# Grouped-query attention on a cached K and V: units of two kv heads made units of four, with 2 MiB loads and VectorE transposes

## Chip, cores and metric

The kernel runs on one core of a Trainium2 chip. The metric is the device time of one execution in microseconds (us). Engines are named as in the profile: PE (TensorE, matmul), PEld (its weight loads), DVE (VectorE), ACT (ScalarE), POOL (GpSimd), SP (SyncE, which issues nearly all DMAs here).

## What is computed

```python
B, Sq, D = 8, 4, 512
Hq, Hkv, Sk, Dh = 32, 8, 2048, 128        # all bf16
q = (x @ wq).reshape(B, Sq, Hq, Dh).transpose(0, 2, 1, 3)
k = jnp.repeat(k_cache, 4, axis=1)        # k_cache, v_cache: (B, Hkv, Sk, Dh)
v = jnp.repeat(v_cache, 4, axis=1)
scores = jnp.einsum("bhqd,bhkd->bhqk", q, k) * (Dh ** -0.5)
p = softmax(scores, axis=-1)
o = jnp.einsum("bhqk,bhkd->bhqd", p, v)
out = o.transpose(0, 2, 1, 3).reshape(B, Sq, Hq * Dh) @ wo
```

Per kv head and batch there are only 16 queries (4 query heads of 4 tokens), so the 64 MiB of K and V cross from memory once and little is computed on each byte. wq and wo are 4 MiB each.

## The kernel before

**Units and loads.** A unit is one batch and a pair of kv heads, 32 units in all (L104). Its K tile and its V tile are 1 MiB each: 128 partitions, 64 for each of the two heads, and on each partition 32 consecutive keys of 128 elements, an 8 KiB run in memory (L108, L118). All loads are issued by SP in the order of the list `loads` (L148): K of unit u, then V of unit u-2, with small pieces of the first wo rows between them. Seven K buffers and six V buffers bound how far ahead `load_ready` (L160) may go. wo's first 1024 rows come in pieces of their own: `wo_e` (L128; eight pieces of five rows of 8 KiB), `wo_m` and `wo_n` (L135); the other 3 MiB come as `wo_sb` in eight loads after the last V (L141, called at w == NU-1-VB).

**K transposes.** `transpose_part` (L193) takes a quarter of a K tile. Two neighbouring bf16 values are seen as one fp32 word, so a 128x128 fp32 transpose on PE moves 128x256 values; four of them fill a PSUM tile, and DVE copies it to SBUF as `kt` (L200), 128x1024 bf16. Even and odd elements of a head's 128 dimensions then lie on 64 partitions each way, and the two kv heads of a unit lie on the two halves of the columns.

**q.** 128 matmuls of 32 columns (L220) make q for all heads, ACT scales it (L227), four matmuls with a selection matrix (L236) sort even and odd dimensions, and copies on DVE and ACT write the block-diagonal `q_bd` (L245).

**Scores and softmax.** `scores` (L254) runs 16 matmuls of 256 columns on four column groups of PE; ACT takes the exponential in two parts with a running sum each (L272). Nothing is subtracted first.

**Probabilities.** `probs_to_keys` (L277) transposes them back with four PE matmuls (L280), and two ACT copies out of PSUM (L286) place each head's 64 partitions into a zeroed `probs` tile, so that one value matmul serves both heads.

**Values.** `values` (L316) runs 32 matmuls of 32 columns with a 128x128 V block as weights (L321). `norms` (L293), every second unit, adds the sums over partitions with a matmul by ones (L303) and takes the reciprocal on DVE (L311); `finish` (L330) multiplies into `oT` (L332).

**Output.** `to_tokens` (L340) and `to_wo_rows` (L363) bring a group of heads into the order of wo's rows with PE transposes and copies (L345, L351, L367, L369), and `project` (L387) multiplies by wo (L397). Group 0 and group (1, 2) are done inside the loop; most of group 0's projection too. After the loop come the third group's transposes and 48 projection matmuls, then an ACT copy (L453) and two output DMAs.

**Order.** The order on every engine is the order of the program (`manual_schedule`, L71). The loop (after `project`) does, for step n: two K quarters of unit n, scores of n-1, the other two quarters, values, norms and finish of n-2, probs_to_keys of n-1.

Of the kernel before, what the change touches and what calls it, by code (L numbers as in the profile page):

```python
# [14 lines left out]
def kernel(  # L15
# [9 lines left out]
    nc = tc.nc  # L25
# [8 lines left out]
    G2 = Hkv // 2  # L34
    C = 2 * Sk // 128
    NQ = 2 * rep * Sq
    HQ = rep * Sq
    J = C // 2
    JT = J // 4
    HP = 2 * rep  # L40
    scale = float(Dh) ** -0.5
    NU = G2 * B
    KB = 7
    VB = 6
    A = 2
    KA = A + 1
    WR = HP
    DH = D // 2


    NE, WE, WM, WN = 40, 8, 5, 64
    assert NE * WE + 128 * WM + WN == HP * 128
    AX = mybir.AxisListType.X
    ADD = mybir.AluOpType.add
    assert Dh == 128 and C == 32 and NQ == 32 and G2 == 4

    const = ctx.enter_context(tc.tile_pool(name="const", bufs=1))
    wpool = ctx.enter_context(tc.tile_pool(name="wpool", bufs=1))
    kpool = ctx.enter_context(tc.tile_pool(name="kpool", bufs=KB))
    vpool = ctx.enter_context(tc.tile_pool(name="vpool", bufs=VB))  # L60
    ktpool = ctx.enter_context(tc.tile_pool(name="ktpool", bufs=6))
    small = ctx.enter_context(tc.tile_pool(name="small", bufs=2))
    psum_k = ctx.enter_context(tc.tile_pool(name="psum_k", bufs=3, space=bass.MemoryType.PSUM))
    psum_s = ctx.enter_context(tc.tile_pool(name="psum_s", bufs=1, space=bass.MemoryType.PSUM))
    psum_t = ctx.enter_context(tc.tile_pool(name="psum_t", bufs=1, space=bass.MemoryType.PSUM))
# [4 lines left out]

    order = ctx.enter_context(tc.manual_schedule())  # L71


    pad0 = const.tile([128, 192], BF16, name="pad0")
    wo_e = const.tile([64, WE, D], BF16, name="wo_e")
    wo_n = const.tile([WN, D], BF16, name="wo_n")
    wo_m = const.tile([128, WM, D], BF16, name="wo_m")
    x_sb = const.tile([T, D], BF16, name="x_sb")
    wq_sb = wpool.tile([128, R, HqDh], BF16, tag="w", name="wq_sb")
    xT_sb = const.tile([128, R, T], BF16, name="xT_sb")  # L80
    qT_all = const.tile([128, G2, B, HP, Sq], BF16, name="qT_all")


    q_bd = const.tile([128, G2, 2, B, 2, 2, HQ], BF16, name="q_bd")
    pick = const.tile([128, 2, 2, Dh // 2], BF16, name="pick")
    ident4 = const.tile([128, 128], FP32, name="ident4")

    groups = [(0,), (1, 2), (3,)]
    oT = [const.tile([128, HP, len(ps), B, Sq], BF16, name=f"oT{ps[0]}") for ps in groups]
    out_sb = const.tile([2 * T, DH], BF16, name="out_sb")  # L90
    oP12 = const.tile([128, WR, 2, T], BF16, name="oP12")
    nat_sb = const.tile([2 * T, HP * 128 + 24 * WE], BF16, name="nat_sb")
    oP3 = const.tile([128, WR, T], BF16, name="oP3")
    oP = [None, oP12[:, :, 0, :], oP12[:, :, 1, :], oP3[:, :, :]]
    oE = const.tile([64, WE, T], BF16, name="oE")
    oM = const.tile([128, WM, T], BF16, name="oM")
    oN = const.tile([WN, T], BF16, name="oN")
    ident = const.tile([128, 128], BF16, name="ident")
    by_q = const.tile([128, HQ], FP32, name="by_q")
    ones = const.tile([128, 128], FP32, name="ones")  # L100
    pad = const.tile([128, 96], BF16, name="pad")
    probs = [const.tile([128, C, 2, HQ], BF16, name=f"probs{i}") for i in range(3)]

    units = [(p, b) for p in range(G2) for b in range(B)]  # L104
    ks = [None] * NU
    vs = [None] * NU

    def load_k(u):  # L108
        if u >= NU:
            return  # L110
        p, b = units[u]
        ks[u] = kpool.tile([128, C, Dh], BF16, tag="k_sb", name="k_sb")
        nc.sync.dma_start(  # L113
            ks[u][:, :, :],
            k_cache[b, 2 * p : 2 * p + 2].rearrange("g (s c) d -> (g s) c d", c=C),
        )

    def load_v(u):  # L118
        if u >= NU:
            return  # L120
        p, b = units[u]
        vs[u] = vpool.tile([128, C, Dh], BF16, tag="v_sb", name="v_sb")
        nc.sync.dma_start(
            vs[u][:, :, :],
            v_cache[b, 2 * p : 2 * p + 2].rearrange("g (s c) d -> (g s) c d", c=C),
        )

    def load_wo_e(i):  # L128

        hi, m = divmod(i, 4)  # L130
        rows = wo[: NE * WE, :].rearrange("(q r) j -> q r j", r=WE)
        a, b = hi * 32 + m, hi * NE // 2 + m
        nc.sync.dma_start(wo_e[a : a + 17 : 4, :, :], rows[b : b + 17 : 4, :, :])

    def load_wo_m():  # L135
        nc.sync.dma_start(wo_n[:, :], wo[HP * 128 - WN : HP * 128, :])
        nc.sync.dma_start(
            wo_m[:, :, :], wo[NE * WE : HP * 128 - WN, :].rearrange("(q r) j -> q r j", r=WM)
        )

    def load_wo(p, r0, n):  # L141
        rows = wo[p * HP * 128 : (p + 1) * HP * 128, :].rearrange("(q r) j -> q r j", r=WR)
        nc.sync.dma_start(wo_sb[:, p - 1, r0 : r0 + n, :], rows[:, r0 : r0 + n, :])

    load_k(0)
    nc.sync.dma_start(wq_sb[:, :, :], wq.rearrange("(p r) n -> p r n", r=R))
    nc.sync.dma_start(x_sb[:, :], x.flatten_outer_dims())
    loads = []  # L148
    for u in range(NU + KA):
        if 1 <= u <= 8:  # L150
            loads.append(("e", u - 1))
        if 0 < u < NU:
            loads.append(("k", u))
        if u == NU + 2:
            loads.append(("m", 0))
        if u >= KA - 1 and u - KA + 1 < NU:
            loads.append(("v", u - KA + 1))
    loads.reverse()

    def load_ready(nk, nv):  # L160

        while loads:
            kind, u = loads[-1]
            if kind in "em":
                loads.pop()
                load_wo_e(u) if kind == "e" else load_wo_m()
                continue
            if u >= (nk + KB if kind == "k" else nv + VB):
                return
            loads.pop()  # L170
            (load_k if kind == "k" else load_v)(u)

    nc.gpsimd.memset(wo_e[:, :, :], 0.0)
    load_ready(0, 0)

    make_identity(nc, ident[:])
    make_identity(nc, ident4[:])
    for e in range(2):
        for g in range(2):
            nc.vector.tensor_copy(  # L180
                out=pick[:, e, g, :], in_=ident[:, :].rearrange("d (k e) -> d e k", e=2)[:, e, :]
            )
    nc.vector.memset(q_bd[:, :, :, :, :, :, :], 0.0)
    for t in probs:
        nc.vector.memset(t[:, :, :, :], 0.0)
    nc.vector.memset(ones[:, :], 1.0)
    nc.vector.tensor_reduce(
        out=by_q[:, :], in_=ident4[:, :].rearrange("p (c q) -> p q c", q=HQ), axis=AX, op=ADD
    )

    kt = {}

    def transpose_part(u, t):  # L193
        kp = psum_k.tile([128, JT, 128], FP32, tag="k", name="kp")
        k4 = ks[u][:, :, :].rearrange("s c d -> s (c d)").bitcast(FP32)
        for j in range(JT):
            w = (t * JT + j) * 128
            nc.tensor.transpose(kp[:, j, :], k4[:, w : w + 128], ident4[:, :])  # L198
        k_t = ktpool.tile([128, JT, 128, 2], BF16, tag="kt", name="kt")
        nc.vector.tensor_copy(  # L200
            out=k_t[:, :, :, :].rearrange("k j s e -> k (j s e)"),
            in_=kp[:, :, :].rearrange("k j s -> k (j s)").bitcast(BF16),
        )
        kt[(u, t)] = k_t
# [281 lines left out]
```

## Time and profile before

| what | us |
|---|---|
| time, median of 3 runs | 190.58 |
| lowest and highest run | 188.97, 190.89 |
| span of the profiled execution | 187.5 |
| PE, PEld, DVE, ACT busy in it | 143.8, 119.1, 108.6, 69.5 |
| bytes moved by DMA | 75.92 MB, mean 405 GB/s |

The span runs from the first to the last instruction of one profiled execution; the run's own time contains that and what lies around it, and is not listed for the profiled execution itself. Busy times overlap between engines. The chain that ended last is followed back from the last instruction: each step names what released it. The slices cut the span in 40 equal parts, each digit being tenths of busy time.

### The profile page before, as it was taken

To read this page: it belongs to the slowest core of one execution; us is meant where nothing else is said; L and a number is where in the kernel's file an instruction comes from. 1 tells how busy PE (TensorE), PEld (TensorE's weight loads), DVE (VectorE), ACT (ScalarE), POOL (GpSimd) and SP (SyncE) were. 2 spreads that over 40 slices of the span, in tenths; PEclk is the share of its full clock that TensorE was granted. 3 is DMA by queue.
4 is the path that set the end of the run, shared out by engine and by line. 5 is a ranking of instruction groups with operands and counts; after the bars stand their busy time and mean duration, and the time that the engine had idled before them with its cause. 6 is when DMAs were issued, how large, how long until landed. Compare 5 with 4: busy or idle time off the path is not lost.

```text
span 187.5 us, 5636 instructions
## 1 busy us (share of the span) xinstructions
PE 143.8 (77%) x2474; PEld 119.1 (63%) x2474; DVE 108.6 (58%) x217; ACT 69.5 (37%) x202; POOL 4.6 (2%) x9
## 2 busy tenths in 40 slices
PE   0516799977879988898788888787787888878493
PEld 0506488866658867786676766566676677667272
DVE  0850698757527766577565657575565666663120
ACT  2001664553324444153344444433344443425200
POOL 8100000000000000000000000000000000000000
PEclk9975999999969999999999999999999999999759
DMA  5999999999999999999999999999999999999970
GB/s 204 467 447 379 421 435 416 425 426 425 425 425 428 421 423 423 430 421 428 425 428 421 428 425 418 428 428 418 430 426 419 425 426 428 419 426 408 409 277 12
DMA packets 10984, 75.92 MB, mean 405 GB/s; under 512 B 1288, under 2 KB 1448, under 8 KB 2600
## 3 DMA queue, kind: packets, MB, share of 16 engines
q1 hardware_dynamic: 10912, 75.55, 96.2%
q8 instruction: 19, 0.31, 0.6%
q14 instruction: 5, 0.04, 0.1%
q10 hardware_dynamic: 48, 0.02, 0.0%
HBM read 75.53 MB, written 0.03 MB: 403 GB/s over the span
## 4 chain that ended last, share of the span: by engine, by line
DMA 92%; PE 6%; SPq 0%; issue 0%; ACT 0%; DVE 0%
DMA k_sb<-in_k_cache_dram 58%; DMA v_sb<-in_v_cache_dram 18%; DMA wo_m<-in_wo_dram 9%; DMA wq_sb<-in_wq_dram 8%; PE out_ps L397 3%; PE kp L198 1%; PE o_ps L321 1%; PE nat L345 0%; SPq L113 0%; PE perm L367 0%; PE s_ps L261 0%; ACT out_sb L453 0%; DVE oT L332 0%
## 5 line engine op out<-in xcount | busy, mean ns | idle before, releaser
L200 DVE COPY kt<-kp 128x1024 bf16<-128x1024 bf16 x128 | 82.3, 685 | 38.6 <-PE kp L198 38.4
L198 PE MATMUL kp<-ident,k_sb 128*128 128x128 f32 x512 | 71.3, 284 | 24.3 <-DMA k_sb<-in_k_cache_dram 22.7
L198 PEld LDWEIGHTS kp<-ident,k_sb 128*128 128x128 f32 x512 | 57.0, 144 | 36.0 <-issue 18.5
L286 ACT COPY probs<-pt 64x512 bf16<-64x512 bf16 x64 | 37.1, 580 | 53.1 <-PE pt L280 52.7
L272 ACT ACTIVATE s_sb<-s_ps 128x256 bf16<-128x256 f32 x64 | 24.0, 380 | 34.1 <-PE s_ps L261 21.7
L321 PE MATMUL o_ps<-probs,v_sb 128*128 128x32 bf16 x1024 | 30.7, 177 | 2.0 <-DMA v_sb<-in_v_cache_dram 1.2
L321 PEld LDWEIGHTS <-v_sb 128*128 128x128 bf16 x1024 | 29.8, 96 | 3.7 <-DMA v_sb<-in_v_cache_dram 2.8
L261 PE MATMUL s_ps<-kt,q_bd 128*32 128x256 bf16 x512 | 20.9, 282 | 0.0
L261 PEld LDWEIGHTS <-q_bd 128*32 128x32 bf16 x512 | 10.6, 95 | 6.2 <-issue 5.4
L311 DVE RECIPROCAL r_sb<-l_ps 128x64 f32<-128x64 f32 x16 | 8.9, 557 | 8.6 <-PE l_ps L303 8.6
L272 ACT ACTIVATION_READ_ACCUMULATOR s_sb<-s_ps 128x1 f32 x64 | 12.7, 198 | 0.0
L280 PE MATMUL pt<-ident,s_sb 128*128 128x128 bf16 x128 | 12.3, 218 | 0.0
L303 PE MATMUL l_ps<-by_gq,ones 128*128 128x64 f32 x32 | 6.9, 297 | 5.2 <-DVE by_gq L296 5.2
L332 DVE TENSOR_TENSOR oT<-o_ps,r_sb 128x32 bf16<-128x32 f32 x32 | 6.1, 191 | 6.5 <-PE o_ps L321 5.9
L303 PEld LDWEIGHTS l_ps<-by_gq,ones 128*128 128x128 f32 x32 | 4.8, 188 | 6.7 <-DVE by_gq L296 4.9
L280 PEld LDWEIGHTS <-s_sb 128*128 128x128 bf16 x128 | 8.8, 104 | 0.2 <-ACT s_sb L272 0.2
L227 ACT ACTIVATE qT_all<-psq 128x256 bf16<-128x256 f32 x4 | 1.5, 385 | 16.6 <-PE psq L220 16.6
L245 DVE CAST q_bd<-pse 64x512 bf16<-64x512 f32 x4 | 2.6, 682 | 4.3 <-PE pse L236 4.3
L296 DVE TENSOR_TENSOR by_gq<-l_sb,by_q 128x64 f32<-128x64 f32 x16 | 3.5, 216 | 2.1 <-ACT s_sb L272 2.1
L397 PE MATMUL out_ps<-wo_sb,oP 128*32 128x256 bf16 x48 | 4.4, 336 | 0.0
L210 PE MATMUL xtp<-ident,x_sb 32*128 32x32 bf16 x4 | 0.3, 192 | 4.8 <-DMA x_sb<-in_x_dram 4.8
L453 ACT CAST out_sb<-out_ps 64x256 bf16<-64x256 f32 x1 | 0.4, 366 | 9.6 <-PE out_ps L397 9.6
(45 smaller groups left out, 43.0 us busy)
## 6 DMA issues: line engine op xcount, KB each, us to landing
k_sb<-in_k_cache_dram SPq DMA_DIRECT2D x32, 1024.0 KB, 19.6
v_sb<-in_v_cache_dram SPq DMA_DIRECT2D x32, 1024.0 KB, 13.3
wq_sb<-in_wq_dram SPq DMA_DIRECT2D x1, 4096.0 KB
wo_sb<-in_wo_dram SPq DMA_DIRECT2D x4, 512.0 KB
wo_sb<-in_wo_dram SPq DMA_DIRECT2D x4, 256.0 KB, 8.1
wo_m<-in_wo_dram SPq DMA_DIRECT2D x1, 640.0 KB
wo_e<-in_wo_dram SPq DMA_DIRECT2D x8, 40.0 KB
wo_n<-in_wo_dram SPq DMA_DIRECT2D x1, 64.0 KB, 18.2
```

The source lines that it names most:

```text
L198: nc.tensor.transpose(kp[:, j, :], k4[:, w : w + 128], ident4[:, :])
L200: nc.vector.tensor_copy(out=k_t[:, :, :, :].rearrange("k j s e -> k (j s e)"), in_=kp[:, :, :].rearrange("k j s -> k (j s)").bitcast(BF16),)
L261: nc.tensor.matmul(s_ps[t * 32 : (t + 1) * 32, :, g, :], lhsT=q_bd[:, p, e, b, g, :, :], rhs=kt[(u, t)][:, :, g * 64 : (g + 1) * 64, e], s ...
L272: nc.scalar.activation(out=s_sb[:, :, g, :], in_=s_ps[:, :, g, :], func=EXP, accum_out=l_sbs[u][:, u % 2, g : g + 1])
L280: nc.tensor.transpose(pt[:, j, :], s_sbs[u][:, j, :, :].rearrange("q g s -> q (g s)"), ident[:, :])
L286: nc.scalar.copy(out=pr[rows, :, g, :], in_=pt[rows, :, :].rearrange("s j (c q) -> s (j c) q", q=HQ),)
L296: nc.vector.tensor_tensor(out=by_gq[:, :, :, :], in0=l_sbs[u][:, :, :].unsqueeze(3).to_broadcast([128, 2, 2, HQ]), in1=by_q[:, :].unsqueez ...
L303: nc.tensor.matmul(l_ps[:, :, :].rearrange("d u q -> d (u q)"), lhsT=ones[:, :], rhs=by_gq[:, :, :, :].rearrange("k u g q -> k (u g q)"), ...
L311: nc.vector.reciprocal(r_sb[:, :, :], l_ps[:, :, :])
L321: nc.tensor.matmul(o_ps[:, :], lhsT=vs[u][:, 2 * (t * JT + j) + c, :], rhs=pr[:, i, :, :].rearrange("s g q -> s (g q)"), start=(i == 0), s ...
L332: nc.vector.tensor_tensor(out=oT[(p + 1) // 2][:, :, (p == 2) * 1, b, :], in0=o_pss[u][:, :].rearrange("d (h s) -> d h s", h=HP), in1=r_sb ...
L397: nc.tensor.matmul(out_ps[half * T : (half + 1) * T, :], lhsT=o, rhs=w[:, half * DH : (half + 1) * DH], start=(p == 0 and r == 0), stop=(p ...
```

## The change

A unit becomes one batch and four kv heads, 16 units (two groups of heads p, eight batches). A head has 32 partitions instead of 64, and 64 consecutive keys on each: runs of 16 KiB, and K and V loads of 2 MiB. All large tiles (K, V, two halves of wq, two halves of wo) share one pool of nine slots of 2 MiB; a load may be issued when a slot has been counted free. The separate first pieces of wo go; wo is loaded after the last V, in two and four loads. The last V comes in two loads.

The work goes by half units h (32 of them; 32 keys of each partition): 16 K transposes in four groups, 8 score matmuls of 512 columns, one exponential of 512 columns. The probabilities are turned by one DVE transpose of 32x32 blocks from SBUF to SBUF, and four ACT copies from SBUF, one per head, place them in `probs`. Value matmuls have 64 columns, 32 per half unit, and both halves add into one PSUM tile. `norms` runs once per unit with two matmuls. q is made by 32 matmuls with 512 columns, scaled by ACT and DVE, and sorted by 16 PE transposes. `to_tokens` and `to_wo_rows` run once per group of 16 heads: for the first after unit 7, for the second after the loop. The whole projection, 64 matmuls in two PSUM tiles on four column groups, comes after that; the last copy becomes a DVE addition of the two.

The core of the diff:

```diff
-    G2 = Hkv // 2
-    C = 2 * Sk // 128
+    G = 4
+    GP = Hkv // G
+    S = 128 // G
+    C = Sk // S
+    J = C // 2
+    JH = J // 2
+    CH = C // 2
+    NU = GP * B
+    NH = 2 * NU
+    SLOTS = 9
...
-    kpool = ctx.enter_context(tc.tile_pool(name="kpool", bufs=KB))
-    vpool = ctx.enter_context(tc.tile_pool(name="vpool", bufs=VB))
-    ktpool = ctx.enter_context(tc.tile_pool(name="ktpool", bufs=6))
+    kv = ctx.enter_context(tc.tile_pool(name="kv", bufs=SLOTS))
+    ktpool = ctx.enter_context(tc.tile_pool(name="ktpool", bufs=2))
...
+    def load_kv(to, of, u, parts, name):
         p, b = units[u]
+        to[u] = slot([128, C, Dh], name)
+        rows = of[b, G * p : G * (p + 1)].rearrange("g (s c) d -> (g s) c d", c=C)
+        n = C // parts
+        for i in range(parts):
+            cs = slice(i * n, (i + 1) * n)
+            nc.sync.dma_start(to[u][:, cs, :], rows[:, cs, :])
...
+    def load_wo(p):
+        wos[p] = slot([128, WR, D], "wo_sb")
+        rows = wo[p * HP * Dh : (p + 1) * HP * Dh, :].rearrange("(q r) j -> q r j", r=WR)
+        cuts = [0, 8, 16] if p < GP - 1 else [0, 8, 12, 14, 16]
+        for a, z in zip(cuts, cuts[1:]):
+            nc.sync.dma_start(wos[p][:, a:z, :], rows[:, a:z, :])
+
+    loads = []
+    for u in range(1, NU):
+        loads.append(lambda u=u: load_kv(ks, k_cache, u, 1, "k_sb"))
+        loads.append(lambda u=u: load_kv(vs, v_cache, u - 1, 1, "v_sb"))
+    loads.append(lambda: load_kv(vs, v_cache, NU - 1, 2, "v_sb"))
+    for p in range(GP):
+        loads.append(lambda p=p: load_wo(p))
...
+    def scores(h):
+        u, hh = divmod(h, 2)
         p, b = units[u]
+        s_ps = psum_s.tile([128, JH, S], FP32, tag="s", name="s_ps")
+        for e in range(2):
+            for g in range(G):
+                nc.tensor.matmul(
+                    s_ps[g * 32 : (g + 1) * 32, :, :],
+                    lhsT=q_bd[:, p, e, g, b, :, :],
+                    rhs=kts[h][:, :, g * S : (g + 1) * S, e],
...
+        nc.scalar.activation(
+            out=s_sbs[h][:, :, :], in_=s_ps[:, :, :], func=EXP, accum_out=l_sbs[u][:, hh : hh + 1]
+        )
...
+    def to_keys(h):
+        pTs[h] = small.tile([128, JH, 2, HQ], BF16, tag="pT", name="pT")
+        nc.vector.transpose(
+            out=pTs[h][:, :, :, :].rearrange("s j c q -> s (j c q)"),
+            in_=s_sbs[h][:, :, :].rearrange("q j s -> q (j s)"),
+        )
+
+    def by_head(h):
+        pr = probs[h % len(probs)]
+        for g in range(G):
+            rows = slice(g * 32, (g + 1) * 32)
             nc.scalar.copy(
                 out=pr[rows, :, g, :],
+                in_=pTs[h][rows, :, :, :].rearrange("s j c q -> s (j c) q"),
             )
...
+    def to_tokens(p, half):
+        n = HP // 2
+        nat = psum_l.tile([T, n, Dh], BF16, tag="l", name="nat")
+        for i in range(n):
             nc.tensor.transpose(
...
+        (nc.scalar.copy if half else nc.vector.tensor_copy)(
+            out=nat_sb[:, half * n * Dh : (half + 1) * n * Dh],
+            in_=nat[:, :, :].rearrange("t h d -> t (h d)"),
+        )
+
+    def to_wo_rows(p):
+        perm = psum_l.tile([128, WR, T], BF16, tag="l", name="perm")
...
+    def odd(p, r):
+        return r % 2 == 1 and (p < GP - 1 or r < WR - 4)
...
+            o, at = (out_odd, 2 * T) if odd(p, r) else (out_ps, 0)
...
+    for h in range(1, NH + 2):
+        fresh = 2 <= h < NH
+        if fresh:
+            transposes(h, 0)
+            transposes(h, 1)
+        if h - 1 < NH:
+            scores(h - 1)
+        if fresh:
+            transposes(h, 2)
+        if h == 1:
+            load_ready(2)
+        if h >= 2:
+            if h % 2 == 1:
+                norms((h - 2) // 2)
+            values(h - 2, 0)
+        if h - 1 < NH:
+            to_keys(h - 1)
+        if fresh:
+            transposes(h, 3)
+        if h >= 2:
+            values(h - 2, 1)
+        if h - 1 < NH:
+            by_head(h - 1)
+        if h >= 2 and h % 2 == 1:
+            u = (h - 2) // 2
+            finish(u)
+            if units[u] == (0, B - 1):
+                for half in range(2):
+                    to_tokens(0, half)
+                to_wo_rows(0)
+
+        load_ready((h < NH and h % 2 == 1) + (h >= 2 and h % 2 == 1))
...
+    to_tokens(1, 0)
+    to_tokens(1, 1)
+    to_wo_rows(1)
+    out_ps = psum_e.tile([2 * T, DH], FP32, tag="e", name="out_ps")
+    out_odd = psum_o.tile([128, DH], FP32, tag="o", name="out_odd")
+    project(0, 0, WR)
+    project(1, 0, WR - 4)
+    nc.scalar.copy(out=odd_sb[:, :], in_=out_odd[2 * T :, :])
+    project(1, WR - 4, 4)
...
+    nc.vector.tensor_tensor(out=out_sb[:, :], in0=out_ps[:, :], in1=odd_sb[:, :], op=ADD)
```

## The prediction, as it was put on record

> **What bounds the kernel now.** I read the busy table and the slices first, then the chain that ended last, then the groups of instructions, and last the end of the run in short windows. Busy table, slices and chain shares of the page:
>
> ```profile
> PE 143.8 (77%) x2474; PEld 119.1 (63%) x2474; DVE 108.6 (58%) x217; ACT 69.5 (37%) x202; POOL 4.6 (2%) x9
> ...
> DMA  5999999999999999999999999999999999999970
> GB/s 204 467 447 379 421 435 416 425 426 425 425 425 428 421 423 423 430 421 428 425 428 421 428 425 418 428 428 418 430 426 419 425 426 428 419 426 408 409 277 12
> ...
> DMA 92%; PE 6%; SPq 0%; issue 0%; ACT 0%; DVE 0%
> ```
>
> The DMA engines are full from the second slice to the last but one, at about 425 GB/s, and no compute engine is over 77%: the loads set the pace. The chain in order of time shows how the run ends:
>
> ```profile
> 159.04 17.10 DMA wo_m<-in_wo_dram
> 176.14 0.04 issue
> 176.18 1.58 PE out_ps L397 x12
> 177.76 0.98 PE o_ps L321 x32
> ...
> 178.77 0.20 DVE oT L332
> ...
> 181.50 2.98 PE out_ps L397 x40
> ...
> 184.51 0.37 ACT out_sb L453
> ```
>
> The last bytes of wo land at 183.3 (the trace's packet records), the last matmul ends at 184.5: compute runs out just behind the loads. What counts is therefore when the last loads land, and how long the work behind the last V tile is. The groups that price it (columns: line, engine, operation, tiles, shapes, count | busy us, mean ns | idle before, releaser):
>
> ```profile
> L200 DVE COPY kt<-kp 128x1024 bf16<-128x1024 bf16 x128 | 82.3, 685 | 38.6 <-PE kp L198 38.4
> ...
> L286 ACT COPY probs<-pt 64x512 bf16<-64x512 bf16 x64 | 37.1, 580 | 53.1 <-PE pt L280 52.7
> L272 ACT ACTIVATE s_sb<-s_ps 128x256 bf16<-128x256 f32 x64 | 24.0, 380 | 34.1 <-PE s_ps L261 21.7
> L321 PE MATMUL o_ps<-probs,v_sb 128*128 128x32 bf16 x1024 | 30.7, 177 | 2.0 <-DMA v_sb<-in_v_cache_dram 1.2
> ...
> L311 DVE RECIPROCAL r_sb<-l_ps 128x64 f32<-128x64 f32 x16 | 8.9, 557 | 8.6 <-PE l_ps L303 8.6
> ```
>
> ACT's probs copies have long idle time in front (52.7 us on PE's transposes), so today they are cheap. And the end in windows (span, then busy time and count by engine, granted clock, DMA share, GB/s):
>
> ```profile
> 181.50:183.00 1.50, 1.50 (x18) 1.11 (x20) 0.29 (x1) 0.00 (x0) 0.00 (x0) 0.55 0.35 132
> 183.00:184.60 1.60, 1.46 (x28) 1.07 (x22) 0.00 (x0) 0.09 (x1) 0.00 (x0) 1.00 0.02 8
> ```
>
> 18 projection matmuls took 1.5 us at a granted clock of 0.55, 28 took 1.6 us at 1.00: 83 against 57 ns each.
>
> **Loads: what the change gains.** In the trace's packet records an 8 KiB packet takes 309 ns, a 32 KiB one (wq) 1213 ns, 4 KiB 159, 2 KiB 84, and the 4-byte completion of each load 9 ns. No 16 KiB load is shown; between the 8 and 32 KiB rows it is 309 + 904/3 = 610 ns (bounds 606, half of 1213, and 618, twice 309). A 2 MiB load puts 8 such packets on each of 16 engines: 8 x 610 + 9 = 4.89 us, against 2 x (8 x 309 + 9) = 4.96 now. Over 32 of them that is 2.3 us. wo loses its pieces on five engines (wo_e) and its 5 and 1 KiB rows: per engine 24 x 309 + 8 x 159 + 16 x 84 + 54 = 10.1 us against 10.3 now. Per engine after: 32 x 4.89 + 9.78 (wq) + 10.1 = 176.4, plus 1.3 for the 19 instruction and 11 table fetches, from 2.15 (first packets) gives 179.9, and the slowest engine 0.9 later: 180.8. The same sum for the kernel before gives 182.5 where the records show 181.4 to 183.3. So the last byte lands some 2.5 us earlier.
>
> SP's queue: landing takes 19.6 us now because eight 1 MiB loads stand in line. After, SP waits in order for a slot (K of unit u+5 stands behind V of u+3), nine slots hold up to 40 us of loads; unless compute falls some 25 us behind, no load starts late, and this costs nothing.
>
> **Steady work.** A half unit (one pass h) has 4.89 us of load. PE: 16 transposes 1.7 us (8 in 0.85), 0.17 gap, scores 0.57 (the same columns on four column groups), values 32 x 28 ns = 0.9 us by the L321 row with 32 columns. With 64 columns a value matmul can cost no less than 28 ns and no more than the 55 ns of L280's 128 columns; I take 29, near the lower row, since the same 128x128 weights are loaded and 128 columns hide that load entirely. The 128 L280 transposes go. Odd passes add two norm matmuls (0.32) and PE's wait for by_gq, which now sits behind three kt copies on DVE; values and the next transposes are queued behind it: some 0.8 to 1.0 us. A pair: 4.0 + 4.85 = 8.8 us of the loads' 9.8. DVE: 8 x 0.645 + two 32x32 transposes + 0.28 + 0.56 + 0.23. No DVE transpose is in the trace; for 512 columns the bounds are 0.49 (the 512-word memset, L185) and 1.33 (two of L245's casts of 512 columns, 0.68); I take 0.66, one pass, near that cast: 7.6 us per pair. ACT: one exp of 512 columns, 0.58 like L286's 512 columns and 0.11 of the 0.20 us sum read that follows and is not overlapped, 0.69; and four copies of 32x512. Bounds for a copy: 0.29 (half the area of L286) and 0.65; time goes by columns (128x256 takes 0.38, 64x512 takes 0.58), so 0.60 each, 2.4 per pass, where two copies of 0.585 do it now: 6.2 us per pair. Beside the loads that is hidden; behind the last loads it is not.
>
> [...]
>
> to_tokens(0) and to_wo_rows(0) come inside pass 17 with PE waiting for each copy: 5.8 us, regained at 1.0 per pair by unit 13 or 14: free, but all spare is used. q: wq's second half lands at 17.5 (15.3 now), q ends near 25 (22.5 now); the same slack hides it. POOL's memsets end before 8 us, under the first loads.
>
> **The end.** V14 lands at 2.15 + 33 x 4.93 + 0.7 = 165.5 (4.93 with fetches). PE takes it in pass 30 and ends that at 166.9. Pass 31: two groups of transposes 0.9 and scores(30) 0.6 to 168.4, a third group 0.45 and 0.25 until it is in PSUM, its copy 0.65 to 169.75, by_gq 0.28 to 170.05, the norm matmuls 0.62 to 170.7, reciprocal 0.56 to 171.25, to_keys(30) 0.66 to 172.0 (exp(30) was done at 169.3). From there ACT carries it in order: by_head(30) 2.4 to 174.4, exp(31) to 175.1, to_keys(31) to 175.8, by_head(31) to 178.2, then values(31) 1.1 and finish 0.25: 179.6. V15 (170.5) and wo wait long in SBUF. Then, one after another, as psum_l has one buffer: eight transposes 0.9, DVE copy 0.68 (L351), eight more 0.9, ACT copy of 1024 columns 1.0 (0.58 + 512 columns at 0.20 per 256), 16 transposes 1.2, copy 0.43 (L369), hops: 5.3. Then all 64 projection matmuls, none issued earlier: 36 ns each on four groups at full clock (L261's pace) to 83 ns; PE idled before it, so the clock is low first: 57 ns, 3.6 us (2.3 to 5.3). Latency 0.3, add 0.4, output 2.7 (184.9 to 187.55 now). 179.6 + 12.3 = 191.9. The wo_m wait (2.5 us) and the probs transposes are gone, but lie inside what this replaces.
>
> The profiled span is 187.55, so +4.4. Its own time is not listed; the median of the runs, 190.58, stands 3.0 over the span (1.4 to 3.3 by run), so 195.0.
>
> **Rivals.** (a) Values do not hide their 64 columns: at 55 ns PE needs 10.5 us per pair against 9.8, the lag of pass 17 is never regained, the end is at 201.4, time 204.4; at 42 ns 194, time 197. For: PE then leads; against: L280's four matmuls of 128 columns follow each other at 55 ns with a new 128x128 load each, so the load (28 ns) lies beside the matmul, not behind it. Chance 0.13. (b) DVE's transposes take two passes, 1.33: DVE has 8.9 us of work per pair, and since the fourth kt copy stands behind the transpose and the next scores behind that copy, the pair takes over 10; end 203, time 206. Against: one pass is the plain case. Chance 0.06.
>
> [...]
>
> (c) ACT's copies go by area, 0.29: finish at 177.4, span 189.7, time 192.7, and with the projection at 36 ns 191.4: within 1%. Against: the two ACT rows. Chance 0.12. (d) The loads set the end, faster: the last bytes at 180.8 plus the last matmuls 0.3, latency, add and output give 184.3, time 187.3. It decides if the work from V14 to the last matmul takes under 15.6 us; the rows give 23. For it: before, compute ended 1.2 us behind the loads. Chance 0.07. My case keeps 0.62.
>
> **Numbers.** About 1% (1.9 us) is what a measurement of this kernel can tell from no change. Faster holds (d), 0.07; same holds (c), whose two times lie on both sides of that bound, 0.12; slower holds my case, (a) and (b), 0.81. The range runs from (c) with the fast projection, 191.4, to four fifths of the way into (a), 50 ns a matmul, span 197 and time 200; it leaves out (d), the upper part of (a) and (b), some 0.2. My own case alone runs from 193 (load packets at 606 ns, projection at full clock) to 199 (copies at 0.65, values at 38 ns, projection at 83 ns).
>
> **What would show it.** Right: 16 KiB packets near 610 ns and the last wo byte near 181; by_head near 0.6 each and PE idle on ACT in passes 32 and 33; finish near 179.6; 64 projections after it. Wrong: PE with no idle time from pass 18 on (a), a transpose over 0.9 (b), ACT copies near 0.3 (c), or the last matmul within 2 us of the last landing (d).

## The result, and the profile after

The changed kernel takes 198.62 us (median of 4 runs, 197.85 to 201.96) against 190.63 us (188.97 to 190.89) for the kernel before in the same comparison: a ratio of 1.042, 95% interval 1.036 to 1.049. It is slower, and 3.6 us over the forecast of 195.0, inside the range. The profile shown here is that of a second set of runs of the same kernel, whose execution took 198.25 us with a span of 196.5: in the first profile (span 200.1) the 16 KiB packets took about 680 instead of 611 ns between 20 and 66 us, a slow stretch that some of the traces below have too. The ratios, and the times of the experiments, leave out executions that are longer by some per cent, as some of either kernel are.

Busy table, granted clock, DMA share, rate and chain shares of the page of the changed kernel:

```profile
PE 146.2 (74%) x2036; PEld 113.1 (58%) x2036; DVE 124.0 (63%) x223; ACT 111.4 (57%) x202; POOL 3.8 (2%) x11
...
PEclk9999757699999999999999789999999999997558
DMA  6999999999999999999999999999999999995000
GB/s 200 434 437 427 434 430 427 427 427 430 437 424 429 425 427 430 434 420 430 430 434 427 434 430 427 430 424 434 427 425 430 432 427 415 422 424 233 0 3 8
...
PE 48%; ACT 19%; DVE 18%; DMA 8%; issue 4%; SPq 1%; ACTq 0%; DVEq 0%
```

Before, the DMA engines were full to the end and 92% of the chain was DMA. Now they run dry in the 37th of 40 slices, the last three hold no load at all, and DMA is 8% of the chain. The last byte of wo lands at 181.4, against 183.3 before, and the run goes on for 15 us after it. The granted clock of the last four slices is 0.5 to 0.8; before, it also fell near the end (0.7 and 0.5 in two slices), but was back at 1.00 for the last 28 matmuls.

The same middle stretch of both, span of the window, then busy time of PE, PEld, DVE, ACT and POOL, granted clock, DMA share and GB/s; first the changed kernel, then the kernel before:

```profile
60.00:160.00 100.00, 84.73 (x1258) 66.85 (x1255) 77.22 (x139) 69.32 (x126) 0.00 (x0) 0.98 1.01 429
```

```profile
60.00:160.00 100.00, 83.95 (x1472) 70.05 (x1465) 65.32 (x132) 40.96 (x125) 0.00 (x0) 1.00 1.01 425
```

The loads run 1% faster. PE has 214 matmuls fewer and is as busy as it was; DVE has 12 us more in these 100, ACT 28 more. What the change took from PE (the 128 probs transposes) went to DVE and ACT.

The groups that the prediction had to price without a row (busy us, mean ns, idle before):

```profile
L245 ACT COPY probs<-pT 32x512 bf16<-32x512 bf16 x128 | 78.8, 616 | 39.2 <-DVE pT L236 38.1
...
L280 PE MATMUL o_ps<-probs,v_sb 128*128 128x64 bf16 x1024 | 41.1, 195 | 8.5 <-ACT probs L245 6.3
...
L236 DVE STREAM_TRANSPOSE pT<-s_sb 128x512 bf16<-128x512 bf16 x32 | 21.9, 685 | 11.6 <-ACT s_sb L228 11.6
```

A copy of 32 partitions by 512 columns takes ACT 0.62 us, the transpose takes DVE 0.68; the value matmul's 195 ns overlap, as 16 of them follow each other in 0.47 (29 ns each).

PE's waits from 60 to 168 us, engine and line, then what it waited for, in total, times, longest:

```profile
PE l_ps L262 <- DVE by_gq L254: 10.8, 11, 1.0
PE o_ps L280 <- ACT probs L245: 3.1, 10, 0.3
...
```

No V tile and no K tile is in that list: in this stretch every load is there before PE asks for it. The values of the even passes start at 63.54, 72.54, 81.53, 90.52 and 99.52, that is 8.99 us a pair, PE's own pace, while the loads take 9.95 (V8 to V14). And the pass in which the first 16 heads are turned (PE's timeline: start, us, what, idle before):

```profile
99.52 0.63 PE L280 MATMUL o_ps<-probs,v_sb 128*128 128x64 bf16 x16 [0.31 <-ACT probs L245]
...
106.68 0.62 PE L301 MATMUL nat<-ident,oT 128*32 128x128 bf16 x8 [0.52 <-DVE oT L290]
108.07 0.61 PE L301 MATMUL nat<-ident,oT 128*32 128x128 bf16 x8 [0.77 <-DVE nat_sb L306]
109.77 1.17 PE L315 MATMUL perm<-ident,nat_sb 32*128 32x32 bf16 x16 [1.09 <-ACT nat_sb L306]
...
114.47 0.63 PE L280 MATMUL o_ps<-probs,v_sb 128*128 128x64 bf16 x16
```

From 99.52 to 114.47 are 14.95 us, 5.96 more than a pair. Last, the end of the chain in order of time (start, us, what):

```profile
174.27 0.58 DVE pT L236
...
174.87 0.62 ACT probs L245
...
176.76 0.62 ACT probs L245
...
177.39 0.60 ACT s_sb L228
...
178.24 0.72 DVE pT L236
...
180.87 0.62 ACT probs L245
...
181.53 1.88 PE o_ps L280 x32
...
183.71 1.05 PE nat L301 x8
...
186.57 1.01 ACT nat_sb L306
...
188.80 0.33 PE out_ps L326 x2
...
191.91 0.86 PE out_ps L326 x8
```

The kernel before started its last values at 177.7 and had only the last projections behind the last byte (183.3); now there is one long series of pieces on ACT, DVE and PE in turn. V14 lands at about 167.0 (166.9 in this trace's landing records; in two kernels below PE waits for it until 167.0), so this series is 29.5 us long, and the last wo byte (181.4) falls into the middle of it.

### The profile page after: what moved, and what is told of

It reads as the page before. It is cut to its first block, busy times and chain, and to the rows that moved or that the text cites. A ratio compares the mean times of both kernels' runs of the same rounds, so it can differ in the third digit from the quotient of the medians.

```text
span 200.1 us, 4726 instructions
## 1 busy us (share of the span) xinstructions
PE 146.9 (73%) x2036; PEld 113.7 (57%) x2036; DVE 124.9 (62%) x223; ACT 111.4 (56%) x202; POOL 3.8 (2%) x11
## 4 chain that ended last, share of the span: by engine, by line
DMA 45%; PE 29%; ACT 11%; DVE 10%; issue 2%; SPq 1%; DVEq 0%
DMA v_sb<-in_v_cache_dram 37%; PE kp L159 11%; ACT probs L245 9%; DMA x_sb<-in_x_dram 8%; PE o_ps L280 6%; DVE kt L160 3%; PE l_ps L262 3%; PE s_ps L218 3%; DVE pT L236 3%; DVE r_sb L270 2%; PE out_ps L326 2%; PE nat L301 2%; PE perm L315 1%; ACT nat_sb L306 1%; PE psq L180 1%
## 5 line engine op out<-in xcount | busy, mean ns | idle before, releaser
L245 ACT COPY probs<-pT 32x512 bf16<-32x512 bf16 x128 | 78.8, 616 | 42.9 <-DVE pT L236 41.8
L159 PE MATMUL kp<-ident,k_sb 128*128 128x128 f32 x512 | 79.9, 294 | 8.6 <-DMA k_sb<-in_k_cache_dram 8.6
L280 PE MATMUL o_ps<-probs,v_sb 128*128 128x64 bf16 x1024 | 41.3, 195 | 12.0 <-ACT probs L245 5.2
L280 PEld LDWEIGHTS <-v_sb 128*128 128x128 bf16 x1024 | 39.4, 101 | 15.9 <-issue 9.2
L236 DVE STREAM_TRANSPOSE pT<-s_sb 128x512 bf16<-128x512 bf16 x32 | 21.9, 684 | 11.3 <-ACT s_sb L228 11.3
L228 ACT ACTIVATE s_sb<-s_ps 128x512 bf16<-128x512 f32 x32 | 19.1, 597 | 5.0 <-PE s_ps L218 4.2
L262 PE MATMUL l_ps<-by_gq,ones 128*128 128x64 f32 x64 | 10.5, 287 | 15.4 <-DVE by_gq L254 15.4
L218 PE MATMUL s_ps<-kt,q_bd 128*32 128x512 bf16 x256 | 21.0, 405 | 0.4 <-DVE kt L160 0.4
L218 PEld LDWEIGHTS <-q_bd 128*32 128x32 bf16 x256 | 4.0, 95 | 6.0 <-issue 5.9
L228 ACT ACTIVATION_READ_ACCUMULATOR s_sb<-s_ps 128x1 f32 x32 | 6.5, 203 | 0.4
```

Of the source, the lines that this page charges most:

```text
L218: nc.tensor.matmul(s_ps[g * 32 : (g + 1) * 32, :, :], lhsT=q_bd[:, p, e, g, b, :, :], rhs=kts[h][:, :, g * S : (g + 1) * S, e], start=(e = ...
L228: nc.scalar.activation(out=s_sbs[h][:, :, :], in_=s_ps[:, :, :], func=EXP, accum_out=l_sbs[u][:, hh : hh + 1])
L236: nc.vector.transpose(out=pTs[h][:, :, :, :].rearrange("s j c q -> s (j c q)"), in_=s_sbs[h][:, :, :].rearrange("q j s -> q (j s)"),)
L245: nc.scalar.copy(out=pr[rows, :, g, :], in_=pTs[h][rows, :, :, :].rearrange("s j c q -> s (j c) q"),)
L262: nc.tensor.matmul(l_ps[:, :], lhsT=ones[:, :], rhs=by_gq[:, hh, :, :].rearrange("k g q -> k (g q)"), start=(hh == 0), stop=(hh == 1),)
L280: nc.tensor.matmul(o_pss[u][:, :], lhsT=vs[u][:, hh * CH + i, :], rhs=pr[:, i, :, :].rearrange("s g q -> s (g q)"), start=(hh == 0 and i = ...
```

## The experiments

The theory after the result: the loads did what was forecast; the end is set by compute, which reaches V14 late (a late start, the stall in pass 17) and then has a chain behind V14 that is longer than the loads behind it. Rivals: the longer runs cost something; one single piece (the copies, or the projection) explains it all; or the loads still hold the end in some hidden way. Ratios are to the kernel before on the same chip, with 95% intervals. All kernels compute the whole result.

**The changed kernel again.**

> The changed kernel as it is, for a second profile. Theory (the end is a serial chain behind V14, started late because compute still lags from the stall of pass 17): about 198.5 us, span near 196, last wo byte near 181 where packets take 611 ns throughout, finish of the last unit near 183. Rival A (the 46 us of 681 ns packets in the profile are what the change brings): those packets are there again, and the last byte lands near 186. Rival B (the pass itself is too slow for the loads, 9.0 us a pair being at the limit): PE waits for no V load after pass 8.

198.25 and 196.51 us (spans 196.5 and 194.6), the kernel before 188.7 to 190.9 on the same chip. The result repeats. Packets take 611 ns, the last byte lands at 181.4 and the last unit is finished at 183.7, as the theory has it, and the slow stretch is not there (rival A). Rival B's sign is there, since PE waits for no V load, but not its cause: at 8.99 us a pair PE is faster than the loads, and has only not caught up with them. Two executions of this kernel lie 1.8 us apart; a single edit worth 1 to 2 us is therefore judged by the trace, not by the time alone.

**Shorter runs.** Each 2 MiB load becomes two of 1 MiB, with 8 KiB runs as before; everything else is kept.

```diff
-        loads.append(lambda u=u: load_kv(ks, k_cache, u, 1, "k_sb"))
-        loads.append(lambda u=u: load_kv(vs, v_cache, u - 1, 1, "v_sb"))
+        loads.append(lambda u=u: load_kv(ks, k_cache, u, 2, "k_sb"))
+        loads.append(lambda u=u: load_kv(vs, v_cache, u - 1, 2, "v_sb"))
```

> Every K and V load is issued as two of 1 MiB with 8 KiB runs, all else as changed. Theory: packets 309 ns, the last byte 2.3 us later than with 16 KiB runs, and the time 0 to 2.3 us longer, nearer 1, because compute lags at the end. Rival A (long runs make the slow packets): packets stay at 309 throughout, the last byte earlier than 186 and the time up to 4 us shorter. Rival B: no change in time.

198.21 and 195.70 us, ratio 1.038 (1.025 to 1.051): the same as the changed kernel. PE's pace is 8.99 us a pair here too. This trace has the slow stretch too, with 8 KiB packets (about 350 instead of 309 ns between 20 and 60 us), so long runs are not what brings it. The run length is neither the loss nor a gain that reaches the end: what 16 KiB packets save (8 x 618 against 8 x 611 ns, and one completion, a load) adds up to an estimated 2 us at V14, where PE in the changed kernel comes 1.4 us after the landing.

**The stall spread out.** The turning of the first 16 heads is cut in three, at the ends of passes 18, 19 and 20.

```diff
-            if units[u] == (0, B - 1):
-                for half in range(2):
-                    to_tokens(0, half)
-                to_wo_rows(0)
+        if h in (18, 19):
+            to_tokens(0, h - 18)
+        if h == 20:
+            to_wo_rows(0)
```

> The first group's to_tokens and to_wo_rows are put at the ends of passes 18, 19 and 20, one piece each, instead of all in pass 17. Theory: the 7.1 us that pass 17 loses (4.4 of PE waiting, the rest at half clock) fall to under 2, compute is back on the V loads by pass 22, and the time falls by 2 to 3 us. Rival B (pace): the lag comes from every pass, so the time falls by less than 1 us. Rival C (the end alone, from V14 on, is too long, without any lag): no change, within 0.5 us.

196.52 and 196.94 us, ratio 1.037 (1.027 to 1.047): the time does not separate it from the changed kernel. PE's waits from 60 to 168 us in its trace:

```profile
PE l_ps L262 <- DVE by_gq L254: 11.0, 11, 1.1
PE o_ps L280 <- DMA v_sb<-in_v_cache_dram: 5.7, 6, 1.5
```

PE waits for V loads again. Pass 30 starts at 167.0, when V14 lands, where the changed kernel starts it at 168.43: 1.4 us of lag were still there at its end, the rest of the 6 had been regained. But these 1.4 us are not shown to be the edit's. At pass 4, ahead of it, this execution is already 1.6 us earlier (43.92 for 45.56), with a program that is the same up to there. The windows from 36 to 38 us, first the changed kernel, then this one (granted clock, third from the end):

```profile
36.00:38.00 2.00, 2.00 (x23) 2.00 (x22) 1.07 (x3) 1.52 (x3) 0.00 (x0) 0.50 1.07 459
```

```profile
36.00:38.00 2.00, 2.00 (x32) 1.41 (x29) 1.99 (x4) 1.58 (x3) 0.00 (x0) 1.00 1.02 434
```

With this start and the stall as it was, pass 30 would start at an estimated 166.8 (pass 16 at 97.87, 14.95 to pass 18, six pairs of 8.99), no later than V14. What the edit itself shows is that the turning now costs about 2 us (29.6 us from pass 16 to pass 22, about 0.4 of it in waits for V loads, where three pairs are 27.0) instead of 5.96.

**Half the projection early.** The 32 matmuls of the first 16 heads go into passes 32 and 33, in front of the values, and all add into `out_ps`.

```diff
+        if h == NH:
+            out_ps = psum_e.tile([2 * T, DH], FP32, tag="e", name="out_ps")
+            project(0, 0, WR // 2)
...
+            if h == NH + 1:
+                project(0, WR // 2, WR // 2)
...
-    project(0, 0, WR)
```

> The first group's 32 projection matmuls are issued in passes 32 and 33, in front of value matmuls that wait for ACT there, all into out_ps; 32 stay behind. Theory: PE is idle there, so the 32 cost nothing and 1.8 us leave the end (32 x 57 ns), up to 2.5 if the clock is granted longer. Rival: the matmuls stand in front of the last values and delay them by what they save: within 0.5 us. Rival A or B say nothing of this run.

194.40 and 194.53 us, ratio 1.025 (1.015 to 1.035). From the start of the last values to the end of the span are 12.2 us (184.84 to 197.07) where the changed kernel has 15.0 (181.53 to 196.48). Not all of these 2.7 us are projection that left the tail: from the start of the perm transposes to the end it is 7.7 for 8.9, 1.1 us less. The other 1.6 lie ahead of them, where the two kernels run the same matmuls:

```profile
184.84 1.09 PE L280 MATMUL o_ps<-probs,v_sb 128*128 128x64 bf16 x32 [0.71 <-ACT probs L245]
...
186.25 0.62 PE L301 MATMUL nat<-ident,oT 128*32 128x128 bf16 x8 [0.32 <-DVE oT L290]
```

The same 32 value matmuls took 1.88 us in the changed kernel and the same eight transposes 1.05, at a granted clock of 0.50; here, with matmuls in PE's waits, it is 1.00 from 180 to 188. (This trace has the slow stretch as well, and its V14 lands at 171.7; what is compared lies behind all values' loads.)

**The sums early.** `by_gq` is made at the end of the even pass, ahead of the three kt copies that it stood behind.

```diff
             by_head(h - 1)
+            if h % 2 == 0:
+                sums((h - 1) // 2)
```

> by_gq, the DVE product in front of the norm matmuls, is issued at the end of the even pass instead of in the odd one, so PE no longer waits for it (15.4 us in all). Theory, as the runs so far leave it: in undisturbed runs compute goes at its own pace, 8.99 us a pair, from a late start, and is 2.9 us behind V14 at the end; then 28 us of serial work. It says: the pair falls to about 8.1, compute is held by the V loads again from pass 20 or so, and the time falls by 1.8 (the lag, down to where loads hold it) plus about 1 (the norm chain stands no longer in front of to_keys in pass 31), 2.5 to 3.3 us in all. Rival (something else sets the pair, ACT's copies or DVE): the pair stays over 8.7 and the time falls by 1 us or less.

195.39, 197.16 and 194.88 us, ratio 1.032 (1.022 to 1.042). The trace has the slow stretch, so only passes without a wait for a load are read. Where no load holds it, the pair takes 8.2 to 8.3 instead of 8.99 us (values at 35.36, 43.69, 51.87), and the wait for `by_gq` is gone from PE's waits after 60 us. The prediction had put this wait at 0.8 to 1.0 us in every odd pass; it was 0.98.

**The last copies shared.** In the last two half units two of the four by_head copies go to DVE.

```diff
-            nc.scalar.copy(
+            (nc.vector.tensor_copy if h >= NH - 2 and g % 2 else nc.scalar.copy)(
```

> In the last two half units two of the four by_head copies go to DVE, which is idle there. Theory: ACT's copies stand in series behind V14 (2.5 + exp + 2.5 us), so each half unit's copies take 1.25 instead of 2.5 and the end comes 2.2 to 2.5 us earlier. Rival (DVE's or PE's own chain stands right behind): 1 us or less. A DVE copy from SBUF should take 0.2 to 0.6 us; no run shows it yet.

197.16, 194.87, 194.47 and 196.68 us, ratio 1.029 (1.020 to 1.039). ACT's and DVE's timelines of the last half unit:

```profile
181.24 1.24 ACT L245 COPY probs<-pT 32x512 bf16<-32x512 bf16 x2 [0.78 <-DVE pT L236]
```

```profile
181.30 0.59 DVE L245 COPY probs<-pT 32x512 bf16<-32x512 bf16 x2
```

The same copy takes DVE 0.29 us and ACT 0.62. The chain of 2.5 us becomes 1.24, twice, as the theory has it. From pass 30 to the end of the span are 23.5 us (171.88 to 195.39) where the changed kernel has 28.05 (168.43 to 196.48), 4.5 less; 2.5 of that are the copies, and most of the rest is the clock again: with the shorter waits it is 1.00 until 187, and the last values take 1.10 us and not 1.88.

**x first.** The small load of x goes ahead of K0 and wq.

```diff
+    nc.sync.dma_start(x_sb[:, :], x.flatten_outer_dims())
     load_kv(ks, k_cache, 0, 1, "k_sb")
     load_wq(0)
     load_wq(1)
-    nc.sync.dma_start(x_sb[:, :], x.flatten_outer_dims())
```

> The 32 KB load of x is issued first on SP instead of fourth, behind wq. Theory: q's matmuls start when wq's halves land (13 and 17.5) and not at 19.2, so the first pass starts some 3 us earlier and the lag at V14 is gone but for what the loads hold: 1.5 to 2 us less time, and PE waits for V loads in it. Rival (the start is hidden by the loads, as forecast): less than 0.5 us.

197.47, 196.68, 197.59 and 197.65 us, ratio 1.040 (1.033 to 1.046). The first values start 1.75 us earlier (33.13 for 34.88), pass 16 1.8 (97.71 for 99.52), pass 30 only 0.8 (167.6 for 168.43). One wait for a V load, 0.5 us at pass 16, lies between; the 1.0 us go behind it, in the stall of pass 17 and in pass 18:

```profile
112.87 1.06 PE L280 MATMUL o_ps<-probs,v_sb 128*128 128x64 bf16 x16
...
114.58 0.63 PE L280 MATMUL o_ps<-probs,v_sb 128*128 128x64 bf16 x16
```

The second half of pass 18's values starts 1.71 us after the first, where the changed kernel has 0.93 (114.47 and 115.40): the granted clock is 0.50 from about 108 to 114.5 us here, and from 111 to 114.3 there. Nor is the lead x's alone: at pass 4 this execution (43.55) is 0.4 us ahead of the one with the stall spread out, which loads x late but has no half clock from 36 to 39. What x first is worth by itself is thus not shown; the half clock, which comes at other times in other executions, is as large.

**All four** (stall spread, early projection, early sums, shared copies), in one kernel.

> spread_tokens, early_project, early_sums and last_copies together. Theory: lag 1.8, projection 2.7, copies 2.4 and norm chain 1.0 add, as they lie one behind the other: 7 to 8 us less than the changed kernel, span near 188.5, time near 190.3, level with the kernel before. Rival (the pieces hide behind each other, or the loads hold the end): less than 5 us.

192.17, 193.18, 191.81 and 192.16 us, ratio 1.013 (1.007 to 1.020); the interval lies clear of the changed kernel's. PE waits 15.2 us for V loads after 60 us, pass 30 starts at 166.98 on the landing of V14, and the span is 190.3 us. The gain over the changed kernel's 198.25 and 196.51 is 4 to 6 us, short of the 7 to 8 that the pieces were to add up to. It is still behind, and its end is the chain behind V14 again.

**The tail's two halves side by side.** As all four, with the first half of the last `to_tokens` in one of the kt transposes' PSUM buffers, so that it does not share one buffer with the second half.

```diff
-        nat = psum_l.tile([T, n, Dh], BF16, tag="l", name="nat")
+        first = p and not half
+        nat = (psum_k if first else psum_l).tile([T, n, Dh], BF16, tag="k" if first else "l", name="nat")
```

> The kernel with all four edits, and the first half of the second to_tokens in one of the kt transposes' PSUM buffers, so that its eight transposes and the other half's follow each other and the DVE copy (0.69 us) lies beside the second eight (0.63). Theory (what is left is a serial chain behind the last V tiles): the span falls by the overlapped copy, 0.7 us, from 190.3 to 189.6, time 191.4; the 1.0 us copy on ACT is then alone in the chain. Rival (the projection waits for something else, such as its clock or wo's last bytes): last matmul unchanged, span 190.3.

189.75 to 191.09 us in 8 runs, ratio 1.006 (1.002 to 1.010); the span of the profile is 189.1. From the finish of unit 15 to the end of the perm copy are now 3.84 us (179.19 to 183.03), 0.95 less than in all four (179.42 to 184.21).

**Order in the last two passes.** All four copies of half unit 30 on DVE, so that exp(31) need not stand behind copies on ACT; the sums ahead of the copies; the second quarter of the projection ahead of the norm matmuls.

```diff
-            (nc.vector.tensor_copy if h >= NH - 2 and g % 2 else nc.scalar.copy)(
+            (nc.vector.tensor_copy if h == NH - 2 or h == NH - 1 and g % 2 else nc.scalar.copy)(
...
-            by_head(h - 1)
             if h % 2 == 0:
                 sums((h - 1) // 2)
+            by_head(h - 1)
...
-            if h % 2 == 1:
-                norms((h - 2) // 2)
             if h == NH + 1:
                 project(0, WR // 2, WR // 2)
+            if h % 2 == 1:
+                norms((h - 2) // 2)
```

> The same, and three moves in the last two passes: all four by_head copies of half unit 30 on DVE (4 x 0.29 us), so that exp(31) does not stand behind two copies on ACT (1.24 us); the sums ahead of the by_head copies on DVE (0.30 beside ACT's copies); the second quarter of the projection (0.98 us) ahead of the norm matmuls, where PE waits anyway. Theory: values(31) start at about 175.7 instead of 178.1, the span is 2.0 to 2.4 us under the kernel with the split tail alone, 187.3 to 187.6, time 189.1 to 189.5, level with the kernel before (189 to 190.6). Rival (the V load of unit 14, which lands at 167, and the loads behind it hold the end): span not under 189; or DVE becomes the chain, with eight more pieces of work on it, and the gain is under 1 us.

190.15 to 191.25 us in 7 runs, ratio 1.006 (1.002 to 1.010): no gain. The chain says why (start, us, what):

```profile
147.45 29.06 DMA wo_sb<-in_wo_dram
176.51 0.04 issue
176.55 1.05 PE out_ps L332 x16
177.60 0.59 PE l_ps L267 x4
178.19 0.95 PE o_ps L285 x32
```

The moved matmuls wait for wo's second rows, which land at 176.5, and the norm matmuls and the last values are queued behind them: values(31) start at 178.2, not 175.7. And exp(31) begins at 173.7, as in the kernel ahead of it (173.6), since the scores in front of it wait for their kt copy on DVE: freeing ACT was worth nothing, not 1.2 us. The rival, a wait for loads, decided here, through an order that I had made worse.

**The waits filled.** As the one before, with the early projection where PE only waits and its rows have landed: 16 matmuls behind the values of half unit 30, 16 behind the nat transposes; the nat copies change engines, so that the longer one (ACT) comes first.

```diff
+        if h == NH:
+            out_ps = psum_e.tile([2 * T, DH], FP32, tag="e", name="out_ps")
+            project(0, 0, WR // 2)
         if h >= 2 and h % 2 == 1:
...
     to_tokens(1, 1)
+    project(0, WR // 2, WR // 2)
     to_wo_rows(1)
...
-        (nc.scalar.copy if half else nc.vector.tensor_copy)(
+        (nc.scalar.copy if half != p else nc.vector.tensor_copy)(
```

> The kernel before it (split tail, moves in the last passes), with the first half of the projection's early matmuls put where PE only waits: 16 behind the values of half unit 30 (wo's first rows land at 174.2, and PE stood 0.6 us on them), 16 behind the nat transposes, beside the copy on ACT (wo's second rows land at 176.5, and ahead of the norms they held PE, the norms and the last values 1.2 us); and the two nat copies change engines, the longer one (ACT, 1.0 us) on the half that is ready first. Theory (the serial chain behind V14 is all that is left): values(31) start at 176.4 instead of 178.0, the second nat copy ends at 179.6 instead of 181.55, the last projections start at 181.3, when the last rows of wo have just landed (181.2); span 186.2 to 186.8, time 188.0 to 188.6, level with the kernel before or up to 1% faster. Rival (loads): not under a span of 187.5, since the last rows land at 181.2 and 32 matmuls, at half clock 2.0 us, stand behind them.

188.41 to 191.11 us in 7 runs, five of them under 188.6, against 189.12 to 191.41 for the kernel before on the same chip: ratio 0.994 (0.989 to 0.999). The end of its chain:

```profile
176.24 0.59 PE l_ps L267 x4
176.83 0.95 PE o_ps L285 x32
...
178.08 0.96 PE nat L307 x14
...
180.02 1.14 PE perm L321 x16
...
181.19 0.44 DVE oP L322
...
181.66 0.28 PE out_ps L332 x2
...
182.50 0.45 PE out_ps L332 x8
```

The last projections start at 181.66, 0.4 us after the last byte of wo (181.27): compute and loads end together again, as they did before the change, and the span is 186.7. That is the version that is level with the kernel before, by the interval between 0.1 and 1.1% faster; the 2 us by which the last byte lands earlier come out as about 1. The theory stands: taking apart the chain behind V14, and the lag ahead of it, gave back the whole loss, and no load was touched.

## Why the prediction was right in sign and 3.6 us short

Against the profile with span 196.5 (forecast 191.9), term by term:

| step of the prediction | forecast | measured |
|---|---|---|
| V14 lands | 165.5 | 167.0 |
| its pass starts behind that by | 0 | 1.4 |
| from there to finish(15) | 14.1 | 15.2 |
| finish(15) to the end of the span | 12.3 | 12.85 |
| span | 191.9 | 196.5 |
| time less span | 3.0 | 1.75 |

- **Loads.** 16 KiB packets take 611 ns (610 forecast), the last byte lands at 181.4 (180.8). The step failed only in how V14 stands to it: its last packet ends at 166.6, 14.8 us ahead of the last byte and not 15.3, and PE goes on 0.4 us behind that packet.
- **The lag regained "by unit 13 or 14".** This step failed in the profiled execution, by the 1.4 us of the table: it spent all the slack and put a further delay at nothing. Its two sizes are near: the stall is 5.96 us (5.8), and 0.96 us is regained a pair (1.0), as PE takes 8.99 a pair and not 8.8, but the loads from V8 to V14 take 9.95 and not 9.8. (In PE's sum an even pass takes 3.9 where 4.0 stood, an odd one 5.1 where 4.85 stood; the terms named for an even pass add up to 3.4 only, and the rest is not itemised there.) The late q, said to be hidden by "the same slack", draws on it first. q ends near 30 and not at 25: x lands at 18.4, behind wq, and the two halves are scaled and sorted one after the other (PE stands 3.3 us between the two groups of transposes). By the trace's landing records V1 is there at 38.9, and its values start at 45.56, 6.7 us late; at pass 16 (99.52, V7 at 97.5) 2.0 of that are left. 1.6 of them are the half clock from 36 to 39 us: without it, with the stall spread out, pass 16 comes at 97.87, 0.4 late, and the forecast would have held just so. Behind the stall the lag is 7.3 us (114.47, V8 at 107.2), six pairs regain 5.8, and about 1.5 remain at V14.
- **ACT carries the end.** Right: by_head at 0.62 each (0.60 forecast; its upper bound, 0.65, had no row behind it). The four copies behind each exp took 2.50 where 2.4 stood, twice, 0.2 us.
- **The last values.** 1.1 us forecast, 1.88 measured: the granted clock was 0.5 by then, where the prediction had reckoned with a low clock for the projection alone; with matmuls or shorter copies in front of them they took 1.09 and 1.10. Together with the copies this is nearly the whole 1.1 us of the third row.
- **The tail.** 64 projections took 4.0 us (3.6), at half clock (0.50 from 188 to 190), and the first eight nat transposes 1.05 (0.9). The prediction had the range and took its middle.
- **Time less span.** 1.7 to 1.9 us in all runs here; the prediction took 3.0 from the median of the runs against one profiled span. That hid, by luck, 1.2 us of the other misses: the span was 4.6 us off, the time 3.6.
- **Rivals.** (a) fell: 64 columns cost 29 ns (though the 28 ns taken for 32 columns are 25 from one to the next in the trace before). (b) fell: one DVE transpose takes 0.68 us, near the 0.66 that was taken and half of the 1.33 of this rival. (c) fell: a copy of 32x512 takes 0.62 us, not 0.29. (d) fell in the changed kernel, whose last matmul comes 11 us behind the last byte; its condition, less than 15.6 us from V14 to the last matmul, is not quite met even in the last experiment (166.8 to 182.9, 16.1), whose span is the nearest to (d)'s. Two sums here are a little off and change nothing: (c)'s copies bring finish to 177.1 and not 177.4, and (d)'s terms add up to 184.5 and not 184.3.

What stays open: why executions of the changed kernel differ by 1.8 us while those of the last experiment mostly agree within 0.1. The half clock at the start, 1.6 us in the execution of 198.25, would fit, since PE waits for no load behind it that could take such a delay up; but the execution of 196.51 has no trace. The slow stretch of the loads is another part elsewhere: the 197.16 us execution of the shared last copies has it.

## What to carry to other kernels

A change that speeds up the loads of a load-bound kernel is paid out only if the work behind the last load stays as short as it was: price the chain from the last big tile to the end, piece by piece and engine by engine, before the steady state. Work that is off the path in the middle (copies on an idle engine, a projection kept for the end, two tiles through one PSUM buffer) is in series there, and can be put into the waits of the last passes; but only behind what has landed: in the kernel with the changed order, 16 matmuls stood until wo's second rows landed at 176.5, and the norm matmuls and the last values, queued behind them, came only at 177.6 and 178.2. A lag in a load-bound loop shrinks by the difference of the two paces, so count how many passes are left, and count that slack once: a late start, a stall and a stretch at half clock draw on the same passes. And work put into PE's waits ahead of the end can pay twice, as it did with half the projection early: the tail lost 1.1 us of projection, and the last values took 1.09 us at a granted clock of 1.00, where they had taken 1.88 at 0.50.

## What was not expected of the hardware

- A 32x512 copy from SBUF to SBUF costs ACT 616 ns, more than a 64x512 copy from PSUM (580), and DVE 287 ns. On ACT fewer partitions save nothing here: from PSUM, 32x1024 takes 1002 ns where 64x512, as many elements, takes 580.
- The granted clock halved after 3 us in which PE was 40% busy, without any long wait. The changed kernel at its end, window by window (span, PE, PEld, DVE, ACT and POOL busy, granted clock, DMA share, GB/s):

```profile
176.00:177.00 1.00, 0.09 (x4) 0.10 (x1) 0.00 (x0) 0.98 (x3) 0.00 (x0) 1.00 1.03 428
177.00:178.00 1.00, 0.58 (x21) 0.58 (x20) 0.00 (x0) 0.97 (x2) 0.00 (x0) 1.00 1.01 412
178.00:179.00 1.00, 0.51 (x18) 0.39 (x14) 0.76 (x2) 0.22 (x2) 0.00 (x0) 1.00 0.70 281
...
180.00:181.00 1.00, 0.29 (x2) 0.13 (x2) 0.56 (x1) 0.98 (x3) 0.00 (x0) 0.50 0.41 145
```

  In the 3 us ahead of the fall at 179 PE was busy for 1.2, its longest wait was 1.3, and from there to the end of the projections the clock stays at 0.50 or little above. What makes the clock fall, no run here shows. It sets the price of what follows: the last 32 projection matmuls took 2.3 us at 0.50 (183.07 to 185.40) with the tail's halves side by side, and 1.3 us at 1.00 (181.66 to 182.95) in the last experiment, where other matmuls fill PE's waits before them (PE busy for 10.8 of the 13 us from 170 to 183).
- A value matmul with 64 columns follows the one before it in 29 ns, against 25 with 32 columns: with 128x128 weights that change each time, twice the columns cost 4 ns.
